# Items' products as two halves of 64 rows, side by side in the array, in two PSUM banks added at the end

## The chip, the core and the metric

The kernel runs on one core of a Trainium2 chip. The metric is the device time of one execution in microseconds. The core's engines are PE (TensorE, matmuls; PEld is its loading of weights), ACT (ScalarE), DVE (VectorE), POOL (GpSimd) and SP (SyncE, here an issuer of DMAs). SBUF is the on-chip memory of 128 partitions, PSUM the eight banks per partition that matmuls accumulate in.

## The reference

Sigmoid attention over 8 batches of 12 heads, 448 tokens and 64 values per head, then a mixture of experts in which each of the 3584 tokens goes to one of 8 experts:

```python
scores = scale * np.matmul(q, k.transpose(0, 1, 3, 2)) - np.log(S)
attn = 1.0 / (1.0 + np.exp(-scores))
...
x = np.ascontiguousarray(attn_out.transpose(0, 2, 1, 3)).reshape(B * S, H * D)
logits = x @ w_gate
expert_idx = np.argmax(logits, axis=1)
...
for e in range(E):
    mask = expert_idx == e
    xe = x[mask]
    h = np.maximum(xe @ w1[e], 0.0)
    ye = h @ w2[e]
    out[mask] = gate_w[mask, None] * ye
```

x has 768 columns (DM), the hidden layer 1024 (DF).

## The kernel before

**Attention and the fixed slots.** The first part of the program computes the attention with 64x64 tiles of the array and, from a certain step on, mixes the experts' products of whole batches into it (function `moe`, lines 230 and 253): a batch of 448 tokens is multiplied with the weights of the expert that most of its tokens chose. The change leaves all of that alone.

**Items.** Tokens whose expert is another one are collected into lists on the chip and computed afterwards in items of 256 rows (`TL`), all of one expert. Two items are written out at the end of the program; a loop behind them takes further items, and it is not entered in these executions. An item is computed by `large`.

Layer 1 makes eight results (`j`, of `KF` = 8): 128 hidden columns by 256 tokens, a sum over six blocks of 128 input columns (`t`, of `KD` = 6). Each number is kept as a high and a low part in fp32r (`whi` and `wlo` of a weight, `xh` and `xl` of a token), and each block takes three products: high by high, high by low, low by high. So a result is 18 matmuls of 128x128 weights against 256 columns (line 947), and the items' products are all of this form. A result is read out of PSUM by ACT, which writes its relu (`hih`, line 952), and then by DVE, which writes the low part (`hil`, line 953). Layer 2 makes six results (`d`, `h`): 128 tokens by 256 output columns, a sum over eight blocks in three products each, 24 matmuls (line 963), read out by one scaling on DVE (`xo`, line 970). Four scatters by GpSimd store the rows; the last one stands at the end of the program.

**PSUM.** Layer 1's results rotate through the two banks of `ps_moe`, layer 2's through the four banks of `ps_m2`, one bank for each result. The transposes of the second item's tokens (`px`, line 928, three groups of four 128x128 matmuls in fp32 between the first item's products) have two banks of their own.

**Weights.** SP loads blocks of weights (`wst`); ACT casts each to its high part (`w1h`, `w2h`, line 149), and the low part is the difference (`w1l`, `w2l`, line 150), taken by GpSimd for layer 1 and by DVE for layer 2 in the items. `wts.ahead` issues these splits: at the start of layer 1's result `j`, blocks up to (3, 4, 5, 6, 7, 9, 11, 13)[j], of which the first eight are layer 1's; in layer 2 between products, as old blocks are released.

**Order.** This stretch is under a manual schedule: each engine takes its instructions in the order in which the code writes them. So what stands behind a waiting instruction on ACT or DVE waits as well.

Of the kernel before, what the change touches and what calls it, by code (L numbers as in the profile page):

```python
# [9 lines left out]
F32 = mybir.dt.float32  # L10
# [8 lines left out]
P = 128  # L19
# [5 lines left out]
def tile_sigmoid_attention_top1_moe(  # L25
# [18 lines left out]
    nc = tc.nc  # L44
# [5 lines left out]
    KD = DM // P  # L50
    KF = DF // P
# [15 lines left out]
    ps_moe = ctx.enter_context(tc.tile_pool(name="ps_moe", bufs=2, space=bass.MemoryType.PSUM))  # L67
# [17 lines left out]
    TL = 2 * P  # L85
# [45 lines left out]
    DW = 2 * P  # L131
# [20 lines left out]
    class Weights:  # L152
# [4 lines left out]
        low = nc.gpsimd  # L157
# [654 lines left out]
    rest = ctx.enter_context(tc.tile_pool(name="rest", bufs=1))  # L812
    ps_x = ctx.enter_context(tc.tile_pool(name="ps_x", bufs=2, space=bass.MemoryType.PSUM))
    ps_m2 = ctx.enter_context(tc.tile_pool(name="ps_m2", bufs=4, space=bass.MemoryType.PSUM))
# [108 lines left out]
    def split_rows(xp, xrs, k2):  # L923
# [5 lines left out]
        for kk in range(2):  # L929
# [2 lines left out]
            nc.scalar.copy(xh, part)  # L932
            nc.vector.tensor_sub(xl, part, xh.bitcast(F32))

    def large(wts, b, rec, xrs, tags, home):

        w0 = b * wts.PARTS
        hts = []
        for j in range(KF):
            wts.ahead(w0 + (3, 4, 5, 6, 7, 9, 11, 13)[j])  # L940
            whi, wlo = wts.parts.pop(w0 + j)
            ps = ps_moe.tile([P, 512], F32, tag="moe", name=f"psi1_{j}")[:, :TL]
            for t in range(KD):
                xh, xl = xrs[t]
                ws = slice(t * P, (t + 1) * P)
                for n, (a, b_) in enumerate(((whi, xh), (whi, xl), (wlo, xh))):
                    nc.tensor.matmul(ps, a[:, ws], b_, start=(t == 0 and n == 0), stop=(t == KD - 1 and n == 2))
                    yield
            if j % 3 == 0:
                two = [hpool.tile([P, 2 * S], F32R, tag=f"h{x}{tags[j // 3]}", name=f"hi{x}_{j}") for x in "hl"]  # L950
            hh, hl = (x[:, j % 3 * TL : (j % 3 + 1) * TL] for x in two)
            nc.scalar.activation(hh, ps, AF.Relu)
            nc.vector.scalar_tensor_tensor(hl, ps, 0.0, hh.bitcast(F32), op0=ALU.max, op1=ALU.subtract)
            hts.append((hh, hl))
        xo = [home(h)[:, :DM] for h in range(2)]
        for d in range(ND):
            for h in range(2):
                ps = ps_m2.tile([P, 512], F32, tag="m2", name=f"psi2_{d}_{h}")[:, :DW]
                for j in range(KF):
                    whi, wlo = (x[:, j % 2 * DW : (j % 2 + 1) * DW] for x in wts.parts[w0 + KF + 4 * d + j // 2])  # L960
                    hh, hl = (x[:, h * P : (h + 1) * P] for x in hts[j])
                    for n, (a, b_) in enumerate(((hh, whi), (hh, wlo), (hl, whi))):
                        nc.tensor.matmul(ps, a, b_, start=(j == 0 and n == 0), stop=(j == KF - 1 and n == 2))
                        yield
                    if h == 1 and j % 2:
                        wts.ahead(w0 + KF + min(NU, 4 * d + j // 2 + 6))
                    if d == ND - 1 and h == 0 and j in (1, 3, 5):
                        wts.ahead(w0 + wts.PARTS + j // 2 + 1)
                to, gate = xo[h][:, d * DW : (d + 1) * DW], rec[:, h, 1:2].bitcast(F32)
                nc.vector.tensor_scalar(to, ps, gate, None, op0=ALU.mult)  # L970
        return xo
# [95 lines left out]
    first = [by_raw[:, n * TL : (n + 1) * TL] for n in range(2 * KD - 2)]  # L1067
# [20 lines left out]
    def run(steps, n):  # L1088
        for _ in range(n):
            next(steps)  # L1090

    item = large(wts, NS, recs_2[0], xrs_0, (0, 2, 4), by_stores)
    for n in range(4):
        run(item, 20)
# [3 lines left out]
    xo = yield_all(item)  # L1098
    puts = []
    item = large(wts, B, recs_2[1], xrs_1, (6, 0, 2), by_stores)  # L1100
    run(item, 2)
    for h in range(2):
# [5 lines left out]
    with tc.If(count > 1, preferred_fallthrough_block=False):  # L1108
        with tc.For_i(1, count) as i, tc.manual_schedule():
            ereg, e_s = expert_reg(i + 1), expert_reg(i + SMALL - 1)  # L1110
            for get in get_rows(item_reg(i + 1), recs_2[2]) + small_rows(item_reg(i + SMALL - 1)):
                get()
            xp = sort_large(2)
            for k2 in range(KD // 2):
                split_rows(xp, xrs_1, k2)
            for n in range(KD + KF):
                small_load(e_s, n)
            ys = yield_all(large(Weights([lambda: ereg]), 0, recs_2[2], xrs_1, (0, 2, 4), by_hidden))
            for h in range(2):
                put_rows(ys, h, recs_2[2], [])  # L1120
            yield_all(small_item())
# [30 lines left out]
```

## Time and profile before

| | us |
|---|---|
| median of three timed runs | 787.34 |
| lowest and highest | 786.72, 789.25 |
| the profiled execution | 785.44 |
| its span, first to last instruction | 783.6 |
| PE busy | 774.7 (99%) |
| PEld, ACT, DVE, POOL busy | 607.2, 387.5, 359.2, 357.2 |
| item 1, PE's stretch | 707.05 to some 742.6 |
| item 2, PE's stretch | some 742.6 to 777.6 |

The page's first table says how long each engine was busy; a row of a timeline gives a start, a duration, the engine, line and operation, the tiles written and read, the shapes and a count of merged instructions, and in brackets the idle time before and what ended it. Matmuls are pipelined, so a row's duration is longer than the distance to the next start. The granted clock of PE is given as a share of full speed.

### The profile page before, as it was taken

The numbers are of one execution on the slowest core, as the hardware profiler recorded it, in microseconds if no ns is written. First come the engines' busy times: TensorE is split into PE (matmuls) and PEld (weight loads), VectorE is DVE, ScalarE is ACT, GpSimd is POOL, SyncE is SP. The second block draws the span as 40 slices with busy tenths as digits, with TensorE's granted clock in tenths as the row PEclk, the third lists the DMA queues.
The fourth block names the chain that finished last, engine by engine and source line by source line (L and its number), as shares of the span: only waits on it lengthen the run. The fifth ranks groups of instructions, "written<-read, shape, count | busy, mean of one in ns | idle before, by whom it ended". The sixth has DMA issues, their size and how long they took to land. (4 is left out here: it accounts for less than half of the span.)

```text
span 783.6 us, 15772 instructions
## 1 busy us (share of the span) xinstructions
PE 774.7 (99%) x5710; PEld 607.2 (77%) x5710; DVE 359.2 (46%) x805; ACT 387.5 (49%) x695; POOL 357.2 (46%) x337
## 2 busy tenths in 40 slices
PE   9999999999999999999999999999999999999996
PEld 5756556687786876967868769677798998999996
DVE  2344555374244562436416373154636482134443
ACT  5877775636436355364543643445523342445342
POOL 8647575152342433522515316054265663764351
PEclk9999999999999999999999999999999999999999
DMA  9776799974848837487475876666176454656671
GB/s 207 162 159 155 175 232 203 204 185 112 178 109 176 207 97 172 106 198 177 106 184 83 181 181 156 159 165 165 38 183 147 138 156 104 201 155 165 192 222 38
DMA packets 311779, 124.08 MB, mean 158 GB/s; under 512 B 209054, under 2 KB 309198, under 8 KB 311696
## 3 DMA queue, kind: packets, MB, share of 16 engines
q1 hardware_dynamic: 305648, 110.80, 60.5%
q0 software_dynamic: 5760, 11.76, 5.4%
q8 instruction: 47, 0.77, 0.4%
q10 hardware_dynamic: 288, 0.46, 0.2%
q14 instruction: 36, 0.29, 0.1%
HBM read 100.89 MB, written 22.47 MB: 157 GB/s over the span
## 5 line engine op out<-in xcount | busy, mean ns | idle before, releaser
L597 ACT ACTIVATE at<-sc,bias_s 128x448 f32<-128x448 f32 x336 | 192.9, 634 | 104.1 <-PE sc L611 103.4
L150 POOL TENSOR_TENSOR w1l<-wst,w1h 128x768 fp32r<-128x768 f32 x72 | 132.8, 1853 | 172.3 <-ACT w1h L149 169.1
L150 POOL TENSOR_TENSOR w2l<-wst,w2h 128x512 fp32r<-128x512 f32 x84 | 108.3, 1316 | 140.6 <-ACT w2h L149 137.7
L611 PE MATMUL sc<-qt,kt 64*64 64x448 f32 x1344 | 166.4, 546 | 0.5 <-DVE qt L581 0.5
L628 PE MATMUL av<-at,vn 64*64 64x448 f32 x1344 | 164.6, 537 | 0.3 <-DMA vn<-in_v_dram 0.3
L230 PE MATMUL ps<-xh,w1h 128*128 128x448 f32 x336 | 124.4, 370 | 0.8 <-ACT xf L643 0.7
L230 PE MATMUL ps<-xl,w1h 128*128 128x448 f32 x336 | 123.5, 368 | 0.0
L230 PE MATMUL ps<-xh,w1l 128*128 128x448 f32 x336 | 123.4, 367 | 0.0
L253 PE MATMUL ps<-hh,w2l 128*128 128x448 f32 x336 | 123.3, 367 | 0.0
L253 PE MATMUL ps<-hl,w2h 128*128 128x448 f32 x336 | 123.2, 367 | 0.0
L253 PE MATMUL ps<-hh,w2h 128*128 128x448 f32 x336 | 123.2, 367 | 0.0
L611 PEld LDWEIGHTS sc<-qt,kt 64*64 64x64 f32 x1344 | 79.6, 189 | 54.6 <-issue 40.3
L628 PEld LDWEIGHTS av<-at,vn 64*64 64x64 f32 x1344 | 61.4, 133 | 61.6 <-issue 48.6
L237 ACT ACTIVATE hh<-ps 128x448 fp32r<-128x448 f32 x56 | 30.6, 546 | 140.7 <-PE ps L230 140.7
L149 ACT CAST w2h<-wst 128x512 fp32r<-128x512 f32 x108 | 64.5, 620 | 69.0 <-PE ps L253 55.1
L487 DVE STREAM_TRANSPOSE xt<-av 128x448 f32<-128x448 f32 x48 | 28.4, 628 | 97.0 <-PE av L628 96.9
L238 DVE SCALAR_TENSOR_TENSOR hl<-ps,hh 128x448 fp32r<-128x448 f32 x56 | 34.4, 614 | 83.2 <-ACT hh L237 83.2
L230 PEld LDWEIGHTS ps<-xh,w1h 128*128 128x128 f32 x336 | 63.1, 188 | 10.8 <-issue 3.7
L253 PEld LDWEIGHTS ps<-hh,w2l 128*128 128x128 f32 x336 | 65.2, 194 | 6.6 <-issue 3.5
L265 DVE TENSOR_TENSOR ps<-ps,gt 128x448 f32<-128x448 f32 x42 | 26.5, 630 | 95.1 <-PE ps L253 95.0
L253 PEld LDWEIGHTS ps<-hl,w2h 128*128 128x128 f32 x336 | 65.2, 194 | 6.2 <-issue 3.2
L253 PEld LDWEIGHTS ps<-hh,w2h 128*128 128x128 f32 x336 | 65.2, 194 | 3.3 <-DVE nw L428 0.2
(160 smaller groups left out, 969.7 us busy)
## 6 DMA issues: line engine op xcount, KB each, us to landing
wst<-in_moe_w_dram SPq DMA_DIRECT2D x72, 384.0 KB, 4.0
wst<-in_moe_w_dram SPq DMA_DIRECT2D x54, 512.0 KB, 4.7
x_tok<-xt SPq DMA_DIRECT2D x64, 168.0 KB, 4.0
qn<-in_q_dram SPq DMA_DIRECT2D x184, 56.0 KB, 2.5
raw<-x_tok SPq DMA_DIRECT2D x28, 336.0 KB, 7.0
out_dram<-ob SPq DMA_DIRECT2D x84, 112.0 KB, 2.6
kn<-in_k_dram SPq DMA_DIRECT2D x104, 56.0 KB, 2.9
kn<-in_k_dram POOLq DMA_DIRECT2D x80, 56.0 KB, 4.0
```

The costliest lines, as they stand in the source:

```text
L149: nc.scalar.copy(hi, st)
L150: eng.tensor_tensor(lo, st, hi.bitcast(F32), op=ALU.subtract)
L230: nc.tensor.matmul(ps[:, :S], a[:, ws], b_, start=(t == 0 and n == 0), stop=(t == KD - 1 and n == 2))
L237: nc.scalar.activation(hh[:, :S], ps[:, :S], AF.Relu)
L238: nc.vector.scalar_tensor_tensor(hl[:, :S], ps[:, :S], 0.0, hh[:, :S].bitcast(F32), op0=ALU.max, op1=ALU.subtract)
L253: nc.tensor.matmul(ps[:, :S], a, b_, start=(j == 0 and n == 0), stop=(j == KF - 1 and n == 2))
L265: nc.vector.tensor_tensor(ps[:, :S], ps[:, :S], gate_rows[b], op=ALU.mult)
L487: nc.vector.transpose(xts[b][:, :, t, :], pv[:, :S].rearrange("p (j s) -> p j s", s=32))
L597: nc.scalar.activation(at, ps[:, :S], AF.Sigmoid, bias=bias_s, scale=SCALE)
L611: nc.tensor.matmul(ps[quarter(g, h), :S], ks, ops[g, "q"][OWN[h]], start=True, stop=True)
L628: nc.tensor.matmul(psv[g][OWN[h], :S], ops[g, "v"][rows, c, :], at[rows], start=(c == 0), stop=(c == KC - 1))
```

## The change

Every product of an item is issued as two matmuls, of rows (partitions) 0 to 63 and 64 to 127 of the same weights and the same moving operand. They go to two tiles of the array, 64 rows by 128 columns each, and accumulate in two PSUM banks. When a result is complete, ACT copies the second bank to SBUF (`low`, a new tile with two buffers), and DVE adds it to the first bank in place. What read the result before reads the first bank then. All banks come from `ps_m2`, layer 1's too: four banks, two for each result, so two results deep. `ps_moe` is no longer used by items.

```diff
+    HALVES = [slice(h * P // 2, (h + 1) * P // 2) for h in range(2)]
+
+    def item_sums(name, n):
+        return [ps_m2.tile([P, 512], F32, tag="m2", name=f"{name}_{h}")[:, :n] for h in range(2)]
+
+    def in_halves(pss, a, b_, first, last):
+        for ps, rows in zip(pss, HALVES):
+            nc.tensor.matmul(ps, a[rows], b_[rows], start=first, stop=last)
+
+    def summed(pss):
+        low = rest.tile([P, TL], F32, tag="low", bufs=2, name="low")[:, : pss[0].shape[1]]
+        nc.scalar.copy(low, pss[1])
+        nc.vector.tensor_add(pss[0], pss[0], low)
+        return pss[0]
...
-            ps = ps_moe.tile([P, 512], F32, tag="moe", name=f"psi1_{j}")[:, :TL]
+            pss = item_sums(f"psi1_{j}", TL)
...
-                    nc.tensor.matmul(ps, a[:, ws], b_, start=(t == 0 and n == 0), stop=(t == KD - 1 and n == 2))
+                    in_halves(pss, a[:, ws], b_, t == 0 and n == 0, t == KD - 1 and n == 2)
                     yield
+            ps = summed(pss)
...
-                ps = ps_m2.tile([P, 512], F32, tag="m2", name=f"psi2_{d}_{h}")[:, :DW]
+                pss = item_sums(f"psi2_{d}_{h}", DW)
...
-                        nc.tensor.matmul(ps, a, b_, start=(j == 0 and n == 0), stop=(j == KF - 1 and n == 2))
+                        in_halves(pss, a, b_, j == 0 and n == 0, j == KF - 1 and n == 2)
                         yield
...
+                ps = summed(pss)
```

On PE, at the first group of transposes in item 1, before (`psi_1` is the bank of layer 1's result 1, `w1h` and `w1l` are weights, `by_raw` and `rxf` hold the tokens' parts; a moving operand stands first behind the arrow; x2 counts rows that read alike):

```order
L947 MATMUL psi_0_8337<-rxf_8021,w1h_0_8256 128x256
L947 MATMUL psi_0_8337<-rxf_8020,w1l_0_8257 128x256
L947 MATMUL psi_1_8366<-by_raw,w1h_1_8276 128x256 x2
L928 MATMUL px_8370<-ident,w2s 128x128 x4
L947 MATMUL psi_1_8366<-by_raw,w1l_1_8277 128x256
```

and now:

```order
L942 MATMUL psi_0_1_8338<-rxf_8021,w1h_0_8256 128x256
L942 MATMUL psi_0_0_8337<-rxf_8020,w1l_0_8257 128x256
L942 MATMUL psi_0_1_8338<-rxf_8020,w1l_0_8257 128x256
L942 MATMUL psi_1_0_8388<-by_raw,w1h_1_8276 128x256
L942 MATMUL psi_1_1_8389<-by_raw,w1h_1_8276 128x256
L942 MATMUL psi_1_0_8388<-by_raw,w1h_1_8276 128x256
L942 MATMUL psi_1_1_8389<-by_raw,w1h_1_8276 128x256
L928 MATMUL px_8395<-ident,w2s 128x128 x4
L942 MATMUL psi_1_0_8388<-by_raw,w1l_1_8277 128x256
L942 MATMUL psi_1_1_8389<-by_raw,w1l_1_8277 128x256
```

Each product stands twice, once for each bank, and the transposes stand between pairs as they stood between products. The same holds on line 942 for layer 2.

On DVE, at the end of layer 1 of item 2 (`w2l_8` is the first split of layer 2's weights, `hil` the low part of a hidden result), before:

```order
L953 SCALAR_TENSOR_TENSOR hil_8917<-psi_4_8926,hih_8916 128x256
L150 TENSOR_TENSOR w2l_8_8954<-wst_8_8841,w2h_8_8953 128x512
L953 SCALAR_TENSOR_TENSOR hil_8917<-psi_5_8957,hih_8916 128x256
L150 TENSOR_TENSOR w2l_9_8979<-wst_8_8841,w2h_9_8978 128x512
L150 TENSOR_TENSOR w2l_10_8985<-wst_9_8868,w2h_10_8984 128x512
L953 SCALAR_TENSOR_TENSOR hil_9008<-psi_6_8988,hih_9007 128x256
```

and now:

```order
L947 TENSOR_TENSOR psi_4_0_9358<-psi_4_0_9358,low 128x256
L969 SCALAR_TENSOR_TENSOR hil_9349<-psi_4_0_9358,hih_9348 128x256
L150 TENSOR_TENSOR w2l_8_9408<-wst_8_9207,w2h_8_9407 128x512
L947 TENSOR_TENSOR psi_5_0_9411<-psi_5_0_9411,low 128x256
L969 SCALAR_TENSOR_TENSOR hil_9349<-psi_5_0_9411,hih_9348 128x256
L150 TENSOR_TENSOR w2l_9_9455<-wst_8_9207,w2h_9_9454 128x512
L150 TENSOR_TENSOR w2l_10_9461<-wst_9_9256,w2h_10_9460 128x512
L947 TENSOR_TENSOR psi_6_0_9464<-psi_6_0_9464,low 128x256
```

The add of each result stands right before its `hil`, behind the splits of the weights; ACT's relu, which needs the add, now stands behind DVE's splits through it.

On ACT at the same place, before:

```order
L952 ACTIVATE hih_9465<-psi_4_9475 128x256
L149 CAST w1h_7_9496<-wst_7_9361 128x768
L149 CAST w2h_8_9502<-wst_8_9390 128x512
L952 ACTIVATE hih_9465<-psi_5_9506 128x256
L149 CAST w2h_9_9527<-wst_8_9390 128x512
```

and now:

```order
L946 COPY low<-psi_4_1_9359 128x256
L968 ACTIVATE hih_9348<-psi_4_0_9358 128x256
L149 CAST w1h_7_9401<-wst_7_9080 128x768
L149 CAST w2h_8_9407<-wst_8_9207 128x512
L946 COPY low<-psi_5_1_9412 128x256
L968 ACTIVATE hih_9348<-psi_5_0_9411 128x256
L149 CAST w2h_9_9454<-wst_8_9207 128x512
```

The copy stands right before the relu, and the relu waits for DVE's add in between; the casts of the next weights stand behind the relu as before.

## Rows read from the trace of the kernel before

**Rows 1.** The page's busy table: us, share of the span, instructions of each engine.
```profile
PE 774.7 (99%) x5710; PEld 607.2 (77%) x5710; DVE 359.2 (46%) x805; ACT 387.5 (49%) x695; POOL 357.2 (46%) x337
```

**Rows 2.** Stretches of the two items: length, busy us (instructions), clock, DMA share, GB/s.
```profile
707.05:741.60 34.55, 34.55 (x291) 34.55 (x290) 18.39 (x33) 17.85 (x34) 12.81 (x7) 1.00 0.62 176
741.60:776.20 34.60, 34.60 (x291) 34.60 (x290) 15.11 (x26) 13.60 (x25) 13.86 (x10) 1.00 0.47 147
```

**Rows 3.** Timeline, the last products and the last scaling: start us, duration us, instruction.
```profile
777.21 0.28 PE L963 MATMUL psi<-w2l,hih 128*128 128x256 f32 x1
...
777.33 0.28 PE L963 MATMUL psi<-w2h,hil 128*128 128x256 f32 x1
777.65 0.48 DVE L970 TENSOR_SCALAR xo<-psi,rec 128x256 f32<-128x256 f32 x1 [2.39 <-PE psi L963]
```

**Rows 4.** Groups by form, the items' transposes: tiles and shapes, count, busy us, mean ns.
```profile
L928 PE MATMUL px<-ident,w2s 128*128 128x128 f32 x12 | 1.8, 272 | 0.0
```

**Rows 5.** Timeline of PE: turns of the queries, two attention sets, a group of transposes.
```profile
7.76 0.99 PE L573 MATMUL turn_q<-ident,qn 64*64 64x64 f32 x28
...
302.87 0.93 PE L628 MATMUL av<-at,vn 64*64 64x448 f32 x8
303.62 0.93 PE L611 MATMUL sc<-qt,kt 64*64 64x448 f32 x8
...
712.27 0.60 PE L928 MATMUL px<-ident,w2s 128*128 128x128 f32 x4
```

**Rows 6.** Groups by form, loads of weights of 64, 128 and 1 columns.
```profile
L628 PEld LDWEIGHTS av<-at,vn 64*64 64x64 f32 x1344 | 61.4, 133 | 61.6 <-issue 48.6 <-ACT at L597 6.8 <-DMA vn<-in_v_dram 1.3
...
L963 PEld LDWEIGHTS psi<-w2h,hih 128*128 128x128 f32 x96 | 18.4, 192 | 0.0
...
L870 PEld LDWEIGHTS pli<-ident,lf 128*1 128x1 f32 x4 | 0.3, 82 | 0.4 <-issue 0.3
```

**Rows 7.** Timeline of PE where 64x64 tiles follow full-array products.
```profile
174.43 0.37 PE L253 MATMUL ps<-hh,w2h 128*128 128x448 f32 x1
174.63 0.37 PE L253 MATMUL ps<-hl,w2h 128*128 128x448 f32 x1
174.93 1.04 PE L611 MATMUL sc<-qt,kt 64*64 64x448 f32 x8
175.79 0.93 PE L628 MATMUL av<-at,vn 64*64 64x448 f32 x8
```

**Rows 8.** Groups by form in the items: ACT and DVE reading PSUM, 256 columns.
```profile
L933 DVE TENSOR_TENSOR rxl<-px,rxh 128x256 fp32r<-128x256 f32 x6 | 2.5, 424 | 3.2 <-ACT rxh L932 3.2
...
L932 ACT CAST rxh<-px 128x256 fp32r<-128x256 f32 x6 | 2.2, 375 | 1.5 <-DVE rxl L933 1.5
```

**Rows 9.** Timeline of ACT, item 2, layer 1: relu of results 4 and 5, casts.
```profile
753.89 0.38 ACT L952 ACTIVATE hih<-psi 128x256 fp32r<-128x256 f32 x1 [1.05 <-PE psi L947]
...
756.05 0.38 ACT L952 ACTIVATE hih<-psi 128x256 fp32r<-128x256 f32 x1 [0.54 <-PE psi L947]
756.33 1.13 ACT L149 CAST w2h<-wst 128x512 fp32r<-128x512 f32 x2
```

**Rows 10.** Timeline of DVE at the same place: splits of weights, hil of result 5.
```profile
755.55 1.92 DVE L150 TENSOR_TENSOR w2l<-wst,w2h 128x512 fp32r<-128x512 f32 x1 [0.81 <-ACT w2h L149]
757.39 0.41 DVE L953 SCALAR_TENSOR_TENSOR hil<-psi,hih 128x256 fp32r<-128x256 f32 x1
757.73 1.28 DVE L150 TENSOR_TENSOR w2l<-wst,w2h 128x512 fp32r<-128x512 f32 x2
```

**Rows 11.** Timeline of ACT, item 1, around the first group of transposes.
```profile
709.40 0.38 ACT L952 ACTIVATE hih<-psi 128x256 fp32r<-128x256 f32 x1 [8.98 <-PE psi L947]
...
710.40 0.38 ACT L932 CAST rxh<-px 128x256 fp32r<-128x256 f32 x1
711.27 0.37 ACT L932 CAST rxh<-px 128x256 fp32r<-128x256 f32 x1 [0.49 <-DVE rxl L933]
711.99 0.39 ACT L952 ACTIVATE hih<-psi 128x256 fp32r<-128x256 f32 x1 [0.35 <-PE psi L947]
```

## The prediction

> **What bounds the kernel now.** I read the page's busy table first: PE is busy for 774.7 of the span's 783.6 us, every other engine for about half of it or less [rows 1]. The reader should see that PE is the path, so a change counts by what it does to the start of the next matmul. Next, the table of stretches over the items, the only part that the change touches: item 1 and item 2 each keep PE busy without a gap, at a granted clock of 1.00, which is the 2.4 GHz level [rows 2]. Then the timeline of PE at the end for the pace: a product starts every 0.12 us [rows 3]. Each item has 8 x 18 and 6 x 24 products, two items 576, so 576 x 0.12 = 69.1 us of the kernel, about the sum of rows 2. A layer 1 result is 18 products, 2.16 us, a layer 2 result 24, 2.88 us. Of a product's 0.120 us, its 256 columns at 2.4 GHz are 0.1067; the other 0.0133 is a price per product.
>
> **The change on PE.** Each of the 576 products becomes a pair of matmuls of 64 rows, and each half loads its own weights. No row shows what such a pair costs; the nearest rows give its ends.
>
> Do two halves run beside each other? The attention's matmuls are 64x64 tiles. Two sets of four of them, 448 columns each, follow each other every 0.75 us [rows 5], 0.376 per set. In the full array the same number form (fp32, in the transposes; the rows write f32 for fp32r too, the code tells them apart) takes 0.60 us for four [rows 5] with one lasting 0.272 [rows 4], so 0.109 per 128 columns. Per column that is 0.84 and 0.85 ns: four tiles together cost what one full matmul costs, so they are concurrent. With two clocks per column both leave a price of only 0.0027 (0.376 less 0.3733, 0.109 less 0.1067). The lower end of a pair is therefore 0.1067 + 0.0027 = 0.109.
>
> Is the load of the weights the bound? Loads last 82, 133 and 192 ns for 1, 64 and 128 columns [rows 6]: 0.8 ns a column over a base of some 81, so 105 to 110 ns of loading per product. It hides under the product today, with little left. Were two halves to load one after the other, the pair would take over 0.2 us. But in the first turns of the queries 28 matmuls of 64 columns, alternating between two tiles, take 0.99 us [rows 5], at most 0.071 per pair, where two loads of 64 columns in a row would be 2 x 0.051 = 0.102. Loads of different tiles overlap.
>
> The price per product remains. fp32 shows 0.0027 in the full array and in tiles alike; the items' form (fp32r) shows 0.0133 in the full array. So the price goes with the form and not with the tile, and I take it as kept: 0.120 a pair, **0 us**. The ends are 0.109, which is 576 x 0.0106 = 6.1 us less, and 0.133, if each half pays its own 0.0133 on a shared stage: 7.7 us more.
>
> A page's rule speaks against the change. The Trainium skill (TensorE: Matmul & The Clock Gate, LDWEIGHTS (loading the stationary operand)) says that a load's time goes with its columns, whatever its rows: half the rows save nothing of a load and the loads double. Rows 6 agree on the columns and show nothing on the rows. Were the loads taken singly, the pair would be 0.21 us and the sum an estimated 52 us higher; the overlap in rows 5 speaks against that.
>
> Changing the tile form has a price. From a 128x128 matmul to the first 64x64 one PE takes 0.30 us where products stand 0.20 apart, and the first two sets take 0.86 [rows 7] instead of 0.75: 0.2 for the entry. Item 1's three groups of transposes, which stay in the full array, cost as much or more each, but in a phase that will wait for ACT anyway (below). **+0.2 us.**
>
> **The end of each result.** Added are a copy on ACT (its like, 256 columns from PSUM, lasts 0.375; I take 0.38) and an add on DVE (its like, PSUM minus SBUF, lasts 0.424) [rows 8], with some 0.035 before each: whatever read the result starts 0.87 us later. For the very last result this lies bare: **+0.87 us**.
>
> In between it costs only where PE waits for a bank. There are four, two per result, so a result needs the banks of the result two before, and DVE's last read of them has 2.16 us from the end of its result. Copy and add 0.87, relu 0.38, hil 0.42 make some 1.7. It fits, until the splits of the weights stand in the queues. Follow item 2 from layer 1's result 4 (counted from 0). Its relu started at 753.89 [rows 9]; now 754.76. Behind it stand ACT's casts w1h and w2h and, released by them, DVE's w2l, which began at 755.55 and took 1.92 because GpSimd was subtracting beside it [rows 10]. All of that moves by 0.87, so w2l ends at 758.34. The add of result 5 stands behind it on DVE, where the change puts it; before, only hil did, and relu 5 started at 756.05 [rows 9], waiting for PE alone. DVE starts its next instruction 0.08 before w2l ends [rows 10]: add 758.26, relu 758.72, hil 759.13 to 759.55. Result 7 needs those banks. PE would reach it at 758.01 and starts at 759.59: a stall of 1.58. Then ACT's two casts behind relu 5 (1.13 for two [rows 9]) end at 760.13, DVE's two w2l (1.28 for two [rows 10]) at 760.93, so add 6 starts at 760.87, relu 761.33, hil ends at 762.16. Result 8 could start 2.16 after result 7, at 761.75, and waits 0.45. After that the ring holds: layer 2's results last 2.88 and have no relu. That is 2.03 per item, **+4.1 us** for two.
>
> Item 1 has three more results that share ACT and DVE with a group of transposed tokens. ACT's round there becomes relu and w1h 1.00, first cast to second 0.87 [rows 11], second cast 0.28, copy 0.38, gaps and add 0.48: 3.01 us, where PE needs 2.59 (relu 709.40 to relu 711.99 [rows 11]). It falls back 0.42 in each of three results; what the ring has to spare takes up part, and result 4 waits 0.15, result 5 0.85: **+1.0 us**, with the changes of form inside it.
>
> Sum: 0 + 0.2 + 0.87 + 4.1 + 1.0 = **+6.1 us** on the profiled execution, 785.4 us of which 783.6 are the span. It lies 1.9 under the median of the three timed runs, 787.3; the forecast stands on the median: 793.4 us.
>
> **Rivals.** (a) The pair costs 0.109 to 0.112, the gain that halves can bring. A faster PE reaches its banks sooner: at 0.109 the same chains give 2 x (1.96 + 0.64) + 1.85 = 7.1 us of stalls in place of 5.1. So -6.1 + 7.1 + 0.87 + 0.2 = +2.1, 789.4 us: not slower by anything that a measurement of this kernel tells from no change, about 0.3% or 2.4 us. It decides below 0.111 a pair. For it speak the tile forms of rows 5, against it the price of the form. The Trainium skill (TensorE: Matmul & The Clock Gate, The mechanism) has tiles start some 4 ns apart and otherwise side by side; by that a pair would be an estimated 0.111, the edge of this rival. (b) Each half pays 0.0133: +7.7, stalls 2.6, the rest 1.3, so +11.6 and 799.0 us. Against it: the overlap in rows 5. (c) The change doesn't do what it says, and the halves run one after the other: 0.24 a pair, +69.1 and the tail, no stalls, 857 us. Rows 5 speak against it, though none of them is fp32r. (d) Faster by over 0.3%: 0.109 a pair and under half of the stalls, 784 us. For it only that my stalls are chains of single rows.
>
> **How the numbers follow.** The forecast (0.113 to 0.126 a pair) 0.55, (a) 0.24, (b) 0.11, (c) 0.05, (d) 0.05. The time is that of the likeliest, 793.4. The range reaches from (a), less a little for the runs' spread, to (b): 788.0 to 799.5; it leaves out (c), (d) and edges. Faster 0.05, the same 0.20 (most of (a)), slower 0.75.
>
> **What would show it.** In PE's timeline, pairs of 64x128 every 0.12 us, both halves within some ns of each other; in each item a gap of PE of 1.6 us before layer 1's result 7 and of 0.4 before layer 2's first, ended by DVE; ACT's relu waiting for DVE; the last scaling 1.2 us after the start of the last product instead of 0.3 [rows 3]. A pace of 0.11 or 0.13 overturns the term of PE; no gaps at those two results, that of the banks.

## The result, and the profile after

The changed kernel takes 793.86 us (median, 793.71 to 794.60) against 787.85 us (786.72 to 789.25) of the kernel before: a ratio of 1.0079, 95% interval 1.0064 to 1.0093, which is 5.0 to 7.3 us slower. The forecast was 793.4 us, its range 788.0 to 799.5.

In the changed kernel's code the pairs of halves are line 942 (before 947 and 963), the new copy on ACT is line 946, the new add on DVE 947, the relu 968, DVE's subtraction behind it (hil) 969, layer 2's scaling 987. The page's busy table, in the form of [rows 1]:

```profile
PE 778.4 (98%) x6286; PEld 610.5 (77%) x6286; DVE 371.8 (47%) x833; ACT 396.3 (50%) x723; POOL 356.8 (45%) x337
```

PE has 576 more matmuls, DVE and ACT 28 more instructions each, as the diff says. PE's busy time rose by 3.7 us only; the rest of what was lost is idle time. It lies in the items. The stretch from the first product's start to the last one's (length, then busy us and instructions of PE, PEld, DVE, ACT, POOL, then clock, DMA share, GB/s):

```profile
708.45:784.50 76.05, 72.88 (x1164) 70.95 (x1164) 45.03 (x86) 40.22 (x86) 26.90 (x16) 1.00 0.51 147
```

Before, the same stretch ran from 707.05 [rows 2] to 777.33 [rows 3], 70.28 us, and PE had no gap. So the items became 5.77 us longer up to the last product's start. When the items begin differs by some microseconds from execution to execution, whatever the change (705.7 to 710.3 in the traces of this study), so below I compare this stretch, and what follows it, and not the spans.

The end, on PE, ACT and DVE, against [rows 3]:

```profile
784.38 0.39 PE L942 MATMUL psi<-w2h,hil 64*128 64x256 f32 x2
784.93 0.37 ACT L946 COPY low<-psi 128x256 f32<-128x256 f32 x1 [2.62 <-PE psi L942]
785.33 0.43 DVE L947 TENSOR_TENSOR psi<-psi,low 128x256 f32<-128x256 f32 x1 [2.03 <-ACTq L1125]
785.80 0.48 DVE L987 TENSOR_SCALAR xo<-psi,rec 128x256 f32<-128x256 f32 x1
```

The row of PE groups two matmuls, the last of which starts at 784.50. The scaling starts 1.30 us behind it, where it started 0.32 behind before: 0.98 us of tail. 5.77 + 0.98 = 6.75 us, and 0.1 lies ahead of the first product (the entry, below); the interval of the timed difference holds the sum, 6.85.

The gaps. All that PE waits for in the items, grouped by what ended it (engine, tile, releaser, us in all, times, longest us); before, this view has no row at all:

```profile
PE psi L942 <- DVE hil L969: 3.2, 4, 1.5
```

Four waits, two per item, all ended by DVE's subtraction: before layer 1's result 7 and before layer 2's first. In item 2, PE at both places:

```profile
762.76 0.39 PE L942 MATMUL psi<-rxh,w1l 64*128 64x256 f32 x2
762.88 0.28 PE L942 MATMUL psi<-rxh,w1h 64*128 64x256 f32 x1
764.65 0.38 PE L942 MATMUL psi<-rxh,w1h 64*128 64x256 f32 x1 [1.50 <-DVE hil L969]
764.65 0.50 PE L942 MATMUL psi<-rxl,w1h 64*128 64x256 f32 x2
764.88 0.40 PE L942 MATMUL psi<-rxh,w1l 64*128 64x256 f32 x2
...
766.79 0.28 PE L942 MATMUL psi<-w2h,hih 64*128 64x256 f32 x1
767.24 0.38 PE L942 MATMUL psi<-w2h,hih 64*128 64x256 f32 x1 [0.17 <-DVE hil L969]
```

The pairs come every 0.12 us, until result 7 begins at 762.88 with one half alone. The other half goes to the other bank and has to wait for it until 764.65, and the next product comes 0.22 behind that. Start to start, the excess over the pace is 1.65 and, at layer 2's first result, 0.33; in item 1 it is 1.42 and 0.40. DVE and ACT at the same time, against [rows 9, 10]:

```profile
761.45 1.93 DVE L150 TENSOR_TENSOR w2l<-wst,w2h 128x512 fp32r<-128x512 f32 x1 [0.81 <-ACT w2h L149]
763.30 0.42 DVE L947 TENSOR_TENSOR psi<-psi,low 128x256 f32<-128x256 f32 x1
764.17 0.42 DVE L969 SCALAR_TENSOR_TENSOR hil<-psi,hih 128x256 fp32r<-128x256 f32 x1 [0.45 <-ACT hih L968]
764.67 1.29 DVE L150 TENSOR_TENSOR w2l<-wst,w2h 128x512 fp32r<-128x512 f32 x2
```
```profile
761.32 0.37 ACT L946 COPY low<-psi 128x256 f32<-128x256 f32 x1
763.75 0.38 ACT L968 ACTIVATE hih<-psi 128x256 fp32r<-128x256 f32 x1 [2.06 <-DVE psi L947]
764.03 1.13 ACT L149 CAST w2h<-wst 128x512 fp32r<-128x512 f32 x2
```

The copy of result 5's lower half ends at 761.69. The add that needs it stands behind a split that holds DVE until 763.38, the relu waits 2.06 for the add, and hil ends at 764.59: 0.06 later PE goes on.

Around a group of transposes in item 1 (before, [rows 5] has one such group):

```profile
710.71 0.40 PE L942 MATMUL psi<-by_raw,w1h 64*128 64x256 f32 x4
711.03 0.66 PE L928 MATMUL px<-ident,w2s 128*128 128x128 f32 x4
711.62 0.39 PE L942 MATMUL psi<-by_raw,w1l 64*128 64x256 f32 x2
711.84 0.41 PE L942 MATMUL psi<-by_raw,w1h 64*128 64x256 f32 x4
```

No row has a releaser: nothing is waited for, but the steps from the halves to the transposes, back, and to the next pair are 0.20 to 0.22 each, and the second transpose comes 0.164 behind the first. Beyond the pace of the products a group costs 0.77 us where it cost 0.43 before, 0.35 more (0.345). The entry, in PE's timeline behind the last product of 448 columns:

```profile
708.15 0.37 PE L253 MATMUL ps<-hh,w2l 128*128 128x448 f32 x1
708.45 0.51 PE L942 MATMUL psi<-by_raw,w1h 64*128 64x256 f32 x4
708.78 0.29 PE L942 MATMUL psi<-by_raw,w1l 64*128 64x256 f32 x2
```

The first pair comes 0.30 behind that product instead of 0.20, and the second pair 0.22 behind the first instead of 0.12.

### The profile page after: what moved, and what is told of

Same layout as the page of the kernel before. It is cut to its first block, busy times and chain, and to the rows that moved or that the text cites. A ratio compares the mean times of both kernels' runs of the same rounds, so it can differ in the third digit from the quotient of the medians.

```text
span 792.0 us, 17004 instructions
## 1 busy us (share of the span) xinstructions
PE 778.4 (98%) x6286; PEld 610.5 (77%) x6286; DVE 371.8 (47%) x833; ACT 396.3 (50%) x723; POOL 356.8 (45%) x337
```

## The experiments

Each runs beside the kernel before on one chip. In the traces I read the stretch from the items' first product to the last one's start, which is 70.29 us in the kernel before (to the ns of its trace):

| kernel | ratio (95%) | stretch, us | more than before |
|---|---|---|---|
| changed kernel | 1.0079 (1.0064 to 1.0093) | 76.06 | 5.77 |
| full_two_banks | 1.0079 (1.0066 to 1.0092) | 75.62 | 5.33 |
| halves_not_added | 1.0022 (1.0013 to 1.0030) | 71.42 | 1.13 |
| halves_layer2 | 1.0018 (1.0009 to 1.0027) | 70.83 | 0.54 |
| six_banks | 1.0097 (1.0083 to 1.0112) | 77.21 | 6.92 |
| six_banks_again | one run | 75.73 | 5.44 |
| splits_later | 1.0051 (1.0033 to 1.0068) | 72.58 | 2.29 |
| six_later | 1.0038 (1.0024 to 1.0051) | 72.00 | 1.71 |
| splits_later_before | 1.0008 (0.9999 to 1.0017) | 70.29 | 0.00 |

All kernels with the add have the tail on top of it. The kernel before itself differs from one set of runs to another (785.01, 784.97 and, for the single runs, 788.32 us), so each kernel is compared with the runs beside it.

**The two parts of the change, apart.** The evacuation without the halves:

```diff
-    def in_halves(pss, a, b_, first, last):
-        for ps, rows in zip(pss, HALVES):
-            nc.tensor.matmul(ps, a[rows], b_[rows], start=first, stop=last)
+    def in_turns(pss, a, b_, k, last):
+        nc.tensor.matmul(pss[k % 2], a, b_, start=(k < 2), stop=(k >= last - 1))
...
-                    in_halves(pss, a[:, ws], b_, t == 0 and n == 0, t == KD - 1 and n == 2)
+                    in_turns(pss, a[:, ws], b_, 3 * t + n, 3 * KD - 1)
...
```

`k` is the product's number within its result; layer 2 is changed in the same way.

> Products of all 128 rows as before, but put by turns into two banks, with the changed kernel's copy and add at the end of each result: the change without its halves. Theory: the gaps are the banks' and not the halves', so they stay, about 3.8 us in two items (without the restarts of 0.1 that halves pay after each), with the tail 1.0 and up to 0.3 in the transposes' phase: +4.8 us, ratio 1.006. Rival (the halves hold the banks longer or start late, and that is the cost): +1 us, the tail alone, ratio 1.0013.

Measured: 791.48 us against 785.01, the ratio of the whole change; the 1.006 that I expected lies below its interval. PE's waits in the items, and the rows where results 4 and 5 of item 1 begin (716.46 and 718.94; a row of two takes in the wait between them):

```profile
PE psi L941 <- DVE hil L968: 3.7, 5, 1.4
...
716.46 0.73 PE L941 MATMUL psi<-by_raw,w1h 128*128 128x256 f32 x2
...
718.94 0.28 PE L941 MATMUL psi<-by_raw,w1h 128*128 128x256 f32 x1
719.88 0.39 PE L941 MATMUL psi<-by_raw,w1h 128*128 128x256 f32 x1 [0.66 <-DVE hil L968]
```

So the second bank, its copy and its add are enough for the whole loss. The gaps before result 7 (1.42 and 1.54 over the pace) and layer 2's first (0.41 and 0.33) are the changed kernel's to about a tenth, and each is followed by the same 0.22: that restart is PE's after a wait, not the halves'. I had expected it to be theirs. New here are 0.22 and 0.82 before results 4 and 5, beside the transposes, where I had expected 0.3 at most; with the restarts that is what the forecast of 4.8 us lacked. In the changed kernel only 0.11 is left before result 5: its PE loses 1.04 in that phase to the switches to the transposes and back, and comes later.

The halves without the evacuation:

```diff
     def summed(pss):
-        low = rest.tile([P, TL], F32, tag="low", bufs=2, name="low")[:, : pss[0].shape[1]]
-        nc.scalar.copy(low, pss[1])
-        nc.vector.tensor_add(pss[0], pss[0], low)
         return pss[0]
```

> Halves into two banks, but the second bank is never read: copy and add are left out, so the lower 64 rows are missing from every result. What is left of the change is PE's: pace, entry, switches. Theory: pairs every 0.120 us, no gap that DVE ends, entry 0.1, switches around item 1's transposes 1.2, no tail: +1.3 us over the kernel before, ratio 1.0017. Rival (halves cost by themselves in places that the trace of the changed kernel hides behind its stalls, or bring 0.009 a pair once nothing waits): +3 us or more, or -4.

Measured: 787.08 against 785.01, 1.0 to 2.4 us slower. The stretch is 1.13 longer: 0.1 of the entry and three groups of transposes at 0.35 more; PE waits for nothing else in it, and pairs come every 0.120. The 1.3 us that I expected lies in the interval. Halves alone cost a little and bring nothing.

**In layer 2 only.**

```diff
-            pss = item_sums(f"psi1_{j}", TL)
+            ps = ps_moe.tile([P, 512], F32, tag="moe", name=f"psi1_{j}")[:, :TL]
...
-                    in_halves(pss, a[:, ws], b_, t == 0 and n == 0, t == KD - 1 and n == 2)
+                    nc.tensor.matmul(ps, a[:, ws], b_, start=(t == 0 and n == 0), stop=(t == KD - 1 and n == 2))
...
-            ps = summed(pss)
```

> Halves, copy and add in layer 2 only; layer 1 keeps its products of 128 rows, its two banks and no add. Theory (the cost sits in layer 1's queues, but for the tail): no wait for banks or for the hidden rows, no switch around the transposes; what stays is the tail of the last result, 1.0 to 1.2 us, and three changes of tile form between the layers at 0.1 each: +1.4 us over the kernel before, ratio 1.0018. Rival (copy and add are dear wherever they stand): layer 2's gaps appear too, +3 us or more.

Measured: 786.24 against 784.97, +1.3, as the theory said. In its trace PE waits for nothing in the items; three changes of form cost some 0.19 each, twice what I expected, and make the 0.54, and the tail, 0.87 here, is the rest. Twelve of the 28 results get their copy and add here at no cost but the last one's.

**What the gaps hang on.** A longer ring:

```diff
+    turn = [0]
+
...
-        return [ps_m2.tile([P, 512], F32, tag="m2", name=f"{name}_{h}")[:, :n] for h in range(2)]
+        turn[0] += 1
+        pool, tag = (ps_m2, "m2") if turn[0] % 3 else (ps_moe, "moe")
+        return [pool.tile([P, 512], F32, tag=tag, name=f"{name}_{h}")[:, :n] for h in range(2)]
```

> The halves and their copy and add stay; only the ring of banks is longer, three results deep (six banks, the two idle ones of the earlier experts added) where the change has two. Theory (banks): the gaps of PE before layer 1's result 7 (1.42 and 1.66 us) and before layer 2's first result (0.40 and 0.33) wait for DVE's last read of the banks two results back; with a third pair of banks that read has 2.16 us more and all of them go, some 4.4 us with the four restarts of 0.1. The time is then about 2.3 us above the kernel before: entry 0.1, switches around the transposes 1.2, tail 1.0; ratio 1.003. Rival (weights): PE waits there for the split parts of the weights, which ACT and DVE make late because the copies and adds stand ahead of them; a longer ring changes nothing and the time stays at +6, ratio 1.008.

Measured: 793.12 against 785.01, no better than the change, as the rival said of the time; but what happened on PE neither theory had. The gaps before result 7 and before layer 2 did go, and others came inside layer 2's first result. PE, DVE and ACT there, in item 1:

```profile
728.90 0.39 PE L946 MATMUL psi<-w2h,hih 64*128 64x256 f32 x2
729.69 0.39 PE L946 MATMUL psi<-w2l,hih 64*128 64x256 f32 x2 [0.41 <-DVE w2l L150]
729.91 0.28 PE L946 MATMUL psi<-w2h,hil 64*128 64x256 f32 x2
731.05 0.39 PE L946 MATMUL psi<-w2h,hih 64*128 64x256 f32 x2 [0.86 <-ACT hih L972]
```
```profile
724.83 0.42 DVE L951 TENSOR_TENSOR psi<-psi,low 128x256 f32<-128x256 f32 x1
...
727.49 0.43 DVE L951 TENSOR_TENSOR psi<-psi,low 128x256 f32<-128x256 f32 x1
...
728.95 1.29 DVE L150 TENSOR_TENSOR w2l<-wst,w2h 128x512 fp32r<-128x512 f32 x2 [0.15 <-ACT w2h L149]
...
730.16 0.43 DVE L951 TENSOR_TENSOR psi<-psi,low 128x256 f32<-128x256 f32 x1
```
```profile
730.62 0.38 ACT L972 ACTIVATE hih<-psi 128x256 fp32r<-128x256 f32 x1 [0.98 <-DVE psi L951]
```

PE now runs on to the products that need what DVE and ACT have not made yet: the low part of a block of w2 (0.67 over the pace) and the hidden rows of result 7 (1.01 for the relu's, 0.11 for hil's). The rows of DVE show why. The adds are 2.66 us apart where PE makes a result in 2.16: a round of copy, add, relu, casts and two splits, in which ACT and DVE wait for each other in turn. Behind the split of 1.9 us each result falls back by a further 0.5. The lateness is a debt in the two queues. With two pairs of banks PE pays it at the bank, with three at the data: the three gaps and their restarts come to 2.1 us in item 1, where the change's two came to 2.0. The rival's word on the weights was a part of the truth, in this kernel, not in the changed one.

The same kernel shows one thing more, behind those gaps (columns as above):

```profile
728.90:731.88 2.98, 1.71 (x20) 1.14 (x18) 2.06 (x4) 1.12 (x3) 0.00 (x0) 1.00 0.78 221
731.88:735.30 3.42, 3.42 (x38) 3.42 (x36) 1.85 (x4) 1.61 (x3) 0.00 (x0) 0.50 0.26 77
735.40:738.80 3.40, 3.40 (x62) 3.40 (x60) 2.56 (x5) 1.52 (x3) 0.00 (x0) 1.00 0.54 160
```

The granted clock, 1.00 with the gaps, is 0.50 for 3.4 us behind them, which is the 1.2 GHz level; pairs come every 0.213 and some 1.5 us are lost. Behind the same gaps of item 2 it stays 1.00. A second look at it:

> The six banks once more, for the stretch at half the clock that its first trace has behind the three gaps of item 1 (granted clock 0.50 for some 3.4 us, 16 pairs at 0.213) and not behind the same gaps of item 2. Theory (the gaps bring it, where the clock is looked at): such a stretch behind the gaps of one or both items again. Rival (a chance of that one execution): none. The gaps themselves are those of the first trace: 0.7, 1.0 and 0.1 us inside layer 2's first result.

Measured: 795.30 against 788.32, one run each. Its trace has the same gaps in both items and no such stretch. So in the two traces it came behind one of four sets of equal gaps; what decides it stays open. It was probably not a chance of that one execution, though. Each execution's mean granted clock is on record: 0.995 in the one with the stretch (793.47 us), 0.998 in the second look, and 0.996, 0.999, 0.995 and 0.994 in the other four timed ones of this kernel (793.12, 792.16, 793.01 and 793.86 us). In the other kernels all but one lie at 0.997 to 1.000; the one, 794.47 us and 0.993, is of the kernel with later splits, below. So three more executions here have probably lost time to the clock, and the ratio of 1.0097 seems to hold about 1 us of that (the median is 793.12, the run at 0.999 took 792.16); no trace of them shows it. Without the stretch the items are 0.3 us shorter than the changed kernel's (75.73 against 76.06). In the changed kernel's trace the clock is 1.00 throughout the items.

Less work in the queue:

```diff
-            wts.ahead(w0 + (3, 4, 5, 6, 7, 9, 11, 13)[j])
+            wts.ahead(w0 + (3, 4, 5, 6, 7, 8, 10, 12)[j])
```

> The halves stay, with two pairs of banks; the first part of w2 is split one result later (behind layer 1's result 5 instead of 4, counted from 0, and the following ones each one part later), so that DVE's subtraction of 1.9 us no longer falls beside GpSimd's subtraction of the last part of w1. Theory (the 1.9 us in DVE's queue ahead of the add): the gap before result 7 goes, that before layer 2's first result shrinks to 0 to 0.3 us in each item: 3 to 4.4 us less than the changed kernel, +2 to +3.5 over the kernel before, ratio 1.0025 to 1.0045. Rival (ACT and DVE have too much to do in layer 1 once copy and add are there): the gaps only move on by one result, to layer 2's first, and the time stays within 1 us of the changed kernel's, ratio 1.007 to 1.009.

Measured: 788.64 against 785.01; 1.0051 is a little above the theory's range, its interval reaches down into it, and by the stretch it is 3.5 us less than the changed kernel, as foretold. DVE around results 5 and 6 of item 2, then PE's waits in the items:

```profile
758.50 0.43 DVE L947 TENSOR_TENSOR psi<-psi,low 128x256 f32<-128x256 f32 x1 [0.85 <-ACT low L946]
759.39 0.42 DVE L969 SCALAR_TENSOR_TENSOR hil<-psi,hih 128x256 fp32r<-128x256 f32 x1 [0.45 <-ACT hih L968]
759.89 1.29 DVE L150 TENSOR_TENSOR w2l<-wst,w2h 128x512 fp32r<-128x512 f32 x2
761.10 0.43 DVE L947 TENSOR_TENSOR psi<-psi,low 128x256 f32<-128x256 f32 x1
```
```profile
PE psi L942 <- DVE hil L969: 0.2, 1, 0.2
```

GpSimd's last subtraction of w1 in item 2, in the changed kernel and here:

```profile
760.98 1.85 POOL L150 TENSOR_TENSOR w1l<-wst,w1h 128x768 fp32r<-128x768 f32 x1 [0.31 <-ACT w1h L149]
```
```profile
757.99 1.85 POOL L150 TENSOR_TENSOR w1l<-wst,w1h 128x768 fp32r<-128x768 f32 x1 [0.31 <-ACT w1h L149]
```

The add of result 5 (758.50) no longer stands behind a split. In the changed kernel the split (761.45 to 763.38) ran beside GpSimd's subtraction and took 1.9; here GpSimd has ended at 759.84 before the first split starts, and the splits take 0.64 each. The gap before result 7 is gone; before layer 2's first, 0.35 and 0.29 are left by the starts of the products (of the two waits the view above lists the longer). The same move in the kernel before, as a control (the same line of diff):

> The kernel before, with the later splits alone: what moving the splits costs or brings by itself. Theory: the kernel before waits for none of these, so no change, ratio 1.000 within 0.002. Rival: the move itself is worth part of the 5 us that it brought to the halves (ratio 0.997 or less), or it costs something that the halves' gain hid (over 1.002).

Measured: 785.81 against 784.97, and the stretch is the same to 0.01 us. The move by itself is worth nothing; it helps where an add stands behind the split.

Both remedies at once (the two diffs above):

> Three pairs of banks and the later splits together. With six banks alone PE no longer waited for banks, but one result later for the hidden rows of results 6 and 7: a round of copy, add, relu, subtraction and two splits takes 2.66 us where PE needs 2.16. Theory (a debt of queue time): the later splits take the 1.9 us out of it, the round of 2.66 leaves 0.5 and 1.0 us of lateness for the adds of results 6 and 7, and layer 2's first result comes to those rows 2.2 and 2.5 us after it began, just late enough; the gaps of 0.35 and 0.29 before layer 2's first result and their restarts go too: 0.8 us less than the later splits alone, +2.5 over the kernel before, ratio 1.003. Rival (the wait only changes its place again): gaps of about the same sum within layer 2's first result, ratio 1.004 to 1.005.

Measured: 787.80 against 784.97, 1.0038, an interval that holds the theory's ratio and the rival's. The gaps before layer 2's first are gone; what is left is 0.11 to 0.13 within it, with a restart, in each item. That lies between the two: with restarts the gaps at layer 2's first result cost 0.83 us with the later splits alone and 0.44 here, and the stretch is 0.6 shorter than with the later splits alone, where the theory had 0.8. Now that the debt is small, the longer ring does help a little, by the stretch; the intervals of the two ratios overlap. By the stretch it is the shortest of the kernels with halves and adds throughout, and it is still slower than the kernel before: the switches and the tail stay.

**What a product costs.** Both matmuls of a pair on the same rows:

```diff
-    HALVES = [slice(h * P // 2, (h + 1) * P // 2) for h in range(2)]
+    HALVES = [slice(0, P // 2) for h in range(2)]
```

> The change with both matmuls of a pair on the upper 64 rows, so that they cannot lie beside each other (the lower rows' part of the sum is left out, the upper one's doubled). It measures what the place in the array is worth. Theory: 0.240 us per pair, no stalls, +70 to +72 us over the kernel before. Rival (the two start side by side because they go to two banks, wherever their rows lie): 0.120, +6.

One half alone, into one bank (and without copy and add):

```diff
-        for ps, rows in zip(pss, HALVES):
+        for ps, rows in zip(pss[:1], HALVES):
```

> Only the upper 64 rows of every product are multiplied, into one bank, with no copy and add: half of the sum is left out. Theory (the second half of a pair is free, and the price of 0.0133 goes with the product whatever its rows): 0.120 us per product as in the kernel before, and +1.3 us over it, as with both halves not added. Rival (the price goes with the rows, or the pair hides it): 0.109 to 0.113, -3 to -5 us.

The kernel before with layer 2's products 512 columns wide:

```diff
-                ps = ps_m2.tile([P, 512], F32, tag="m2", name=f"psi2_{d}_{h}")[:, :DW]
+                ps = ps_m2.tile([P, 512], F32, tag="m2", name=f"psi2_{d}_{h}")
...
-                    whi, wlo = (x[:, j % 2 * DW : (j % 2 + 1) * DW] for x in wts.parts[w0 + KF + 4 * d + j // 2])
+                    whi, wlo = (x[:, : 2 * DW] for x in wts.parts[w0 + KF + 4 * d + j // 2])
...
-                nc.vector.tensor_scalar(to, ps, gate, None, op0=ALU.mult)
+                nc.vector.tensor_scalar(to, ps[:, :DW], gate, None, op0=ALU.mult)
```

> The kernel before, with layer 2's products 512 columns wide, twice the part of w2 that belongs to a result, so that its output isn't the layer's (288 products of 512 columns in place of 256). It measures what the 0.0133 us beyond the columns is. Theory (a price per product of this number form): 0.2133 + 0.0133 = 0.227 us per product, +30.7 us in all. Rival (the load of the weights sets 0.120, and hides under a longer product): 0.2133, +26.9 us. Rival (it goes with the columns, 0.469 ns each): 0.240, +34.6 us.

Two products of each in PE's timeline, in this order:

```profile
799.86 0.40 PE L942 MATMUL psi<-rxl,w1h 64*128 64x256 f32 x2
800.10 0.40 PE L942 MATMUL psi<-rxh,w1l 64*128 64x256 f32 x2
```
```profile
759.93 0.28 PE L942 MATMUL psi<-rxh,w1h 64*128 64x256 f32 x1
760.05 0.28 PE L942 MATMUL psi<-rxl,w1h 64*128 64x256 f32 x1
```
```profile
739.97 0.39 PE L963 MATMUL psi<-w2h,hih 128*128 128x512 f32 x1
740.20 0.39 PE L963 MATMUL psi<-w2l,hih 128*128 128x512 f32 x1
```

On the same rows a pair takes 0.24, one half after the other: 858.17 us, 69.9 over the kernel before (788.32, one run each). On rows of their own it takes 0.12: the place in the array is what puts halves side by side. But a half alone takes 0.120 too, as a product of 128 rows does, so rows have no price and halving them frees nothing. Its stretch, 71.38, is 1.09 longer than the kernel before's, nearly as with both halves not added; the time, 788.31 against 788.32, is one run each and can't show a difference of 1 us. And 512 columns take 0.227, that is 0.2133 and again some 0.0133, to the nanosecond the price per product that the prediction worked out; if the load set the pace, it would be 0.2133. The sum of 288 x 0.1067 is 30.7 us, and the stretch became 30.7 longer; the single run's time gave 32.3. The price is not the same for all products of this number form: the earlier batches' products of 448 columns (line 253) start 0.2035 us apart on average in the kernel before, 0.0168 more than their columns. Why is open.

## Why the prediction was right, point by point

**PE's pace, 0 us.** Right: 0.120 a pair, the same as before to a tenth of a nanosecond on average, and the halves of a pair start mostly 3 to 10 ns apart. The argument was the right one as well: for the products of 256 and 512 columns the price of 0.0133 belongs to the product (wide_layer2), whatever its rows (one_half), and is not paid twice in a pair. Of the load of the weights the traces show these groups, the items' halves in the changed kernel and the transposes in the kernel before:

```profile
L942 PEld LDWEIGHTS psi<-w2h,hih 64*128 64x128 f32 x192 | 28.5, 188 | 0.8 <-DVE hil L969 0.8
```
```profile
L928 PEld LDWEIGHTS px<-ident,w2s 128*128 128x128 f32 x12 | 1.4, 140 | 0.0
```

A load of 64 rows takes 188 ns, one of 128 rows took 192 [rows 6], and the two of a pair mostly start 3 to 10 ns apart, so the extra 52 us that loads taken singly would have cost did not come. The Trainium skill (TensorE: Matmul & The Clock Gate, LDWEIGHTS (loading the stationary operand)) says that rows save nothing of a load. The trace agrees: 188 against 192 ns. The prediction's line of 0.8 ns a column over a base of 81 is not a rule of this trace, though: the transposes' loads of 128 columns last 140 ns, and rows 6 mix number forms and tile forms. The forecast's 0 us does not hang on it; the figures of 0.21 us a pair and 52 us do.

**Entry, 0.2 us.** 0.1 ahead of the first pair and 0.1 behind it: 0.2.

**Tail, 0.87 us.** Measured 0.98. In full_two_banks, halves_layer2, splits_later and six_later it is 0.87, as foretold; in the profiled execution of the changed kernel the copy started 0.1 later behind the last product.

**Bank stalls, 4.1 us.** The largest of the steps, and right in its parts: 1.58 before result 7 of each item was 1.42 and 1.65, 0.45 before layer 2's first was 0.40 and 0.33, 3.80 in all. To that comes what the sum left out, a restart of 0.1 behind each of the four, and full_two_banks shows that it comes without halves too: 4.2 us. The mechanism was the foretold one too: the add stands behind the split of 1.9 us, relu and hil behind the add, and PE waits at the bank for hil. What the runs add concerns the ring. From the prediction's "Result 7 needs those banks" I had concluded, for six_banks, that a longer ring would take the gaps away, and that was wrong. The gaps are a debt of ACT's and DVE's queues (six_banks moves it, splits_later takes most of it away), and the ring only says where PE pays it.

**The transposes' phase, 1.0 us.** The sum was about right, its parts not. Measured are three groups at 0.345 more each, 1.04, and 0.21 before result 5 (0.11 of wait, 0.1 of restart): 1.25. The profile names no releaser for this short wait, but DVE's hil of result 3 ends 0.05 before PE goes on. The step said 0.15 before result 4 and 0.85 before result 5, with the changes of form hidden inside. In full_two_banks, where there are no changes of form, PE waits 0.22 and 0.82 there: the waits were worked out correctly for a PE at its full pace. The changed kernel's PE is held up by the switches first, and comes late enough to wait for little. The step put the cover the wrong way round: the switches hide the waits. What was mis-sized is the change of form, "as much or more each" as 0.2 for a group: it is 0.35, and PE pays it in full. That the sum still came out is in part luck: the switches alone cost 1.04 (halves_not_added) and the waits alone 1.04 without their restarts (full_two_banks), so it made little difference which of the two covers the other.

**The sum.** 6.1 foretold; the terms measured are 0.2 for the entry, 1.25 for the phase, 4.2 for the gaps and 0.98 for the tail, 6.6. To that come 0.1 in one step at 752.10 that no row explains and another 0.1 in steps a few ns over the pace, 6.85 in all. Each term is at its size or a little above it, so between the terms no errors cancel; within the phase's they do. The timed difference is 6.0, with an interval of 5.0 to 7.3. The profiled execution of before lay 1.9 under its median, so differences to that one execution were to come out larger than the timed one, unless they were taken within the items.

**Rivals.** (a), a faster pair, (b), a dearer one, and (c), halves in a row, fall with the pace; same_rows shows that (c) was sized right: 69.9 us over the kernel before, where 69.1 and a tail of 0.87 were foretold. (d) falls with them.

No run points to a version that beats the kernel before. Halves bring no pace (halves_not_added), so each of their costs is a loss, and the smallest set of them that was tried, layer 2 alone, is 0.7 to 2.1 us slower.

## What to carry to other kernels

Splitting a full contraction into row tiles paid nothing here, because the full product's time goes by its columns and a price per product: one half alone took as long as the whole. The second bank is the dear part, since a copy and an add at a result's end stand in the queues of other engines; look for the longest instruction that those queues hold ahead of them, and move that one, before lengthening the ring of banks. A wait that goes away when a buffer is added may come back one step later as a wait for data: ask whether the engine behind it makes its rounds (2.66 us here) as fast as the one that waits (2.16).

## What the runs showed of the hardware that I had not expected

- After each of PE's waits that were read in the items, the next product comes 0.22 us behind the first instead of 0.12, with halves and with full rows alike.
- Going from pairs of 64 rows to 128x128 transposes and back costs 0.35 us more per round trip than between products and transposes that both fill the array (0.77 against 0.43).
- One stretch of 3.4 us at a granted clock of 0.50 came behind two gaps of 0.7 and 1.0 us within 2.2 us, in one of four equal places in two traces. The mean clocks of the other executions of that kernel (0.994 to 0.996 in three of four) suggest that it is not rare; when it comes stays open.
- Once out of step, pairs form anew: after the gap at 762.88 the second half of one product starts beside the first half of the next (764.650 and 764.653 in the trace), at the same pace.
